# FNet mixer with a gated channel MLP: two rows of statistics written by element-wise DMAs, and four transposes placed elsewhere

## Chip, cores and metric

The kernel runs on one core of a Trainium2 chip. Its metric is the device time in microseconds; the kernel before takes 668.16 us, the median of 3 runs (668.14 to 668.18). Engines: TensorE (matmuls, with its weight loads shown on a line of their own), VectorE, ScalarE, GpSimd, and SyncE (SP), which here does nothing but issue DMAs.

## What is computed

The input x has 2048 tokens of 512 channels. It is normalized over the channels (xn); s is the real part of a two-dimensional DFT of xn (channels, then sequence); g is the SiLU of an MLP of the normalized xn; the output is x + s * g.

```python
def _A_ref(x, dft_seq_re, dft_seq_im, dft_hid_re, dft_hid_im):
    a = jnp.einsum("bsd,ed->bse", x, dft_hid_re)
    b = jnp.einsum("bsd,ed->bse", x, dft_hid_im)
    return jnp.einsum("ts,bse->bte", dft_seq_re, a) - jnp.einsum("ts,bse->bte", dft_seq_im, b)

def _B_ref(x, w1, b1, w2, b2):
    y = _layernorm(x, axis=-1)
    h = _gelu(jnp.einsum("bsd,df->bsf", y, w1) + b1)
    return jnp.einsum("bsf,fd->bsd", h, w2) + b2

xn = _layernorm(x, axis=-1)
s = _A_ref(xn, A_dft_seq_re, A_dft_seq_im, A_dft_hid_re, A_dft_hid_im)
g = _silu(_B_ref(xn, B_w1, B_b1, B_w2, B_b2))
return x + s * g
```

All is float32; D = 512 channels, S = 2048 tokens, F = 1792 hidden units.

## The kernel before

**Numbers as two parts.** Every float32 operand of a matmul is split into a high part, rounded by ScalarE (hi), and a remainder, subtracted by VectorE (lo). A product is three matmuls: hi hi, hi lo, lo hi. Names ending in h and l in the profile are these parts.

**Stages.** First the DFT over the channels for 16 tiles of 128 tokens (accumulators pd, later q with seven products in place of eight for the second half of the tokens), then the MLP (h, then m), then the DFT over the sequence (p), which ends with the gate and the output. The change lies in the first stage, in the first 50 us; matmuls of that stage are recorded at L364 and L349 (pd) and L556 (q).

**The first stage.** Tokens are taken as four blocks of 512, in the order of `TB`. In a block of four tiles (i = 0 to 15) the channels have to lie along the partitions. Tiles 0 to 3 are loaded with their tokens along the partitions, centred there (`first_centre`) and turned by TensorE, four transposes a tile into one bank pt (`first_transpose`, L272), which ScalarE rounds (L64) and VectorE subtracts from (L65). The other blocks are loaded already transposed (xT). What has to be subtracted or multiplied there differs along the free axis, so a row of 512 values, the same on all 128 partitions, is wanted: the means of block 1 (row m1), the negated means of blocks 2, 3 and 0 (row n), and the inverse deviations, called factors (row R).

**How a row is made.** The statistics come out as columns, one value per token with the tokens along the partitions: `nm` holds 12 such columns, `rr` 32, of which R takes 16. `rows_turn` (L170) lets TensorE transpose the columns (L174, 128 x n into n x 128 in a bank rp), ScalarE copy the bank (L176, into the one buffer rt) and issue a DMA to DRAM (L178), n rows of 512 bytes. `row_load` (L180) has SP load 512, 1024 or more values of that DRAM row to all partitions (L182). The second kind of user is `centred_load` (L333): SP loads row n twice a tile (L338) and GpSimd adds the transposed input to it by an accumulating DMA (L339); this is for block 0, which the MLP uses again.

**Order.** The program's order is the order of each engine. `dft_mm(i, m)` issues 12 matmuls of tile i with the real (m = 0) or the imaginary (m = 1) matrix; its argument `mid` is called after `at` of them. Before the change the turn of R is called after two matmuls of `dft_mm(5, 0)`, that of n between `dft_mm(4, 0)` and `dft_mm(4, 1)`, and the transposes of tile 3 (the fourth) after eight matmuls of `dft_mm(2, 0)`. The turn of m1 stands ahead of `dft_mm(2, 0)`. `dft_out` has ScalarE scale an accumulator into a buffer e (L375) and puts its store on a list; SP stores (L386) lag four entries behind.

**Users of the rows.** In the loop over the tiles i = 3 to 7, `second_factors` computes `rr` at i = 4 (L132 last); `a_sums` (L501 to L504) and `last_factors` run on VectorE at i = 5; at i = 6 `y_centre` (L477) adds row n to four tiles xT, and at i = 7 `y_scale` (L480) multiplies two of these by row R; ScalarE rounds them to y_1h (L79) and VectorE makes y_1l (L83). The first of the q products (`q_product(1)`, L556) reads the first y as its weights.

**Buffers.** 39 of 4 KB a partition are shared by most of this (`operand`, `guest`), and eight banks of PSUM hold accumulators, transposes and turns.

Of the kernel before, what the change touches and what calls it, by code (L numbers as in the profile page):

```python
# [8 lines left out]
F32 = mybir.dt.float32  # L9
# [3 lines left out]
AF = mybir.ActivationFunctionType  # L13
ALU = mybir.AluOpType

P = 128
# [6 lines left out]
def fnet_mixer_kernel(ctx: ExitStack, tc: tile.TileContext, x, xT, ct, wt, w1, w2, b1, b2, out):  # L23
    nc = tc.nc
# [3 lines left out]
    NK = D // P  # L28
# [9 lines left out]
    dram = ctx.enter_context(tc.tile_pool(name="dram", bufs=1, space=bass.MemoryType.DRAM))  # L38
# [7 lines left out]
    def operand(name):  # L46
        return op.tile([P, 2, W], F32R, tag="op", name=name)
# [5 lines left out]
    def guest(name):  # L53
        return op.tile([P, 2, W], F32, tag="op", name=name)

    def bank(name):
        return psum.tile([P, W], F32, tag="ps", name=name)
# [5 lines left out]
    def split_into(hi, lo, src):  # L63
        nc.scalar.activation(hi, src, AF.Copy)  # L64
        nc.vector.tensor_sub(lo, src, hi.bitcast(F32))  # L65
# [37 lines left out]
    HB = NS // 2  # L103
    rr = consts.tile([P, 4 * HB], F32, name="rr")
# [4 lines left out]
    nm = consts.tile([P, 3 * NC], F32, name="nm")  # L109
# [6 lines left out]
    def stats(mv, t, i):  # L116
        st = small.tile([P, 6], F32, tag="st", name="st")
        nc.vector.bn_stats(st, t)
        nc.vector.bn_aggr(mv[:, i, :], st)
# [28 lines left out]
    def second_factors():  # L148
        for make, at in ((outer, 0), (inner, HB)):
            make(vv[:, at:at + NC], mv1[:, HB:HB + NC, 1], 1.0)  # L150
            make(vv[:, at + NC:at + HB], sq, 1.0 / D)
        rsqrt(rr[:, 2 * HB:], vv, 2 * HB)

    def last_factors():
        nc.vector.tensor_mul(qq, vv[:, :HB], rr[:, 2 * HB:3 * HB])
        nc.vector.tensor_mul(qq, qq, rr[:, 3 * HB:])
        nc.vector.tensor_scalar(nq, qq, -1.0, None, op0=ALU.mult)


    row_st, row_d = {}, {}  # L160
# [9 lines left out]
    def rows_turn(key):  # L170
        st = row_st[key]
        n = st.shape[1]
        ps = bank("rp" + key)
        nc.tensor.transpose(ps[:n, :P], st, ident)  # L174
        sb = small.tile([n, P], F32, tag="rt", bufs=1, name="rt" + key)
        nc.scalar.activation(sb, ps[:n, :P], AF.Copy)  # L176
        row_d[key] = dram.tile([1, n * P], F32, name="rd" + key)
        nc.scalar.dma_start(out=row_d[key].rearrange("a (b p) -> (a b) p", p=P), in_=sb)  # L178

    def row_load(key, n, at=0):  # L180
        t = guest(f"row{key}_{at}")
        nc.sync.dma_start(out=t.rearrange("p a w -> p (a w)")[:, :n * W],  # L182
                          in_=row_d[key][0, at * W:(at + n) * W].partition_broadcast(P))
        return [t[:, q, :] for q in range(n)]
# [23 lines left out]
    def parts(i):  # L208
        return 1 if i else 2

    def x_load(i):
        if i % 2 == 0:
            x_two[i // 2] = guest(f"x{i}")
        xs[i] = x_two[i // 2][:, i % 2, :]
        nc.sync.dma_start(out=xs[i], in_=x[tok(i) * P:(tok(i) + 1) * P, :])
# [5 lines left out]
    def load_w(m, k2):  # L221
        t = room(f"rw{m}{k2}")
        for k in (2 * k2, 2 * k2 + 1):
# [8 lines left out]
                        in_=wt[:, :, 0:P:8, 0:4].rearrange("m k p w -> p (m k) w"))  # L232
# [13 lines left out]
    xt = {}  # L246
# [18 lines left out]
    def first_transpose(i):  # L265
        t = operand(f"xt{i}")
        hi, lo = t[:, 0, :], t[:, 1, :]
        n = D // parts(i)
        for q in range(parts(i)):
            pt = bank(f"pt{i}{q}")  # L270
            for k in range(NK // parts(i)):
                nc.tensor.transpose(pt[:, k * P:(k + 1) * P], xc[i][:, q * n + k * P:q * n + (k + 1) * P], ident)  # L272
            split_into(hi[:, q * n:(q + 1) * n], lo[:, q * n:(q + 1) * n], pt[:, :n])
        for k in range(NK):
            xt[i, k] = (hi[:, k * P:(k + 1) * P], lo[:, k * P:(k + 1) * P])

    xtr = {}

# [33 lines left out]
    def m_turn():  # L312
        rows_turn("m1")
        mrow[1], = row_load("m1", 1)
# [4 lines left out]
    def neg_means(b):  # L319
        nc.vector.tensor_scalar(nm[:, block(NEG[b])], mv1[:, block(b), 0], -1.0, None, op0=ALU.mult)  # L320
# [3 lines left out]
    def act_stats(i):  # L324
        if not squares:
            squares.append(guest("squares"))
        t, = squares
        c = i % NC
        nc.scalar.activation(t[:, 0, :], xs[i], AF.Copy, scale=-1.0 / D, accum_out=nm[:, NC + c:NC + c + 1])
        nc.scalar.activation(t[:, 1, :], xs[i], AF.Square, bias=nm[:, NC + c:NC + c + 1], accum_out=sq[:, c:c + 1])  # L330
# [12 lines left out]
    def dft_mm(i, m, mid=None, at=2 * NK):  # L343
        acc = bank(f"pd{i}_{m}")
        terms = [(0, 0, k) for k in range(NK)] + [(1, 0, k) for k in range(NK)] + [(0, 1, k) for k in range(NK)]
        for n, (px, pw, k) in enumerate(terms):
            if mid and n == at:
                mid()
            nc.tensor.matmul(acc, xt[i, k][px], weights[m * NK + k][pw], start=n == 0, stop=n == len(terms) - 1)  # L349
        dacc[i, m] = acc  # L350
# [20 lines left out]
    def dft_out(i, m):  # L371
        if m == 0:
            e_two[i] = guest(f"e{i}")
        e = e_two[i][:, m, :]
        nc.scalar.activation(e, dacc.pop((i, m)), AF.Copy, scale=(nr1 if m else rr)[:, i:i + 1])  # L375
        stores.append((dft_at(i, m), e))
        while len(stores) > LAG:
            store()
# [11 lines left out]
    round_w(0)  # L390
    rest_w(0)
    first_transpose(0)
    for n in (1, 2, 3, 4, 5):
        round_w(n)
# [11 lines left out]

    idle_mm(1)
    first_mm(lambda: first_transpose(1))
    first_mean(2)
    first_var(1)  # L410
    first_centre(2)
    stats(mv1, xs[NC], NC)
    stats(mv1, xs[NC + 1], NC + 1)
    dft_mm(1, 0, mid=lambda: first_transpose(2))
    first_mean(3)
    first_var(2)
# [4 lines left out]
    m_pack()  # L421
    dft_mm(1, 1)
    m_turn()
    for q in (14, 15, 10, 11):
        x_load(q)
    for q in (12, 13):
# [1 line left out]
    first_factors()  # L428
    for q in (8, 9):
        stats(mv1, xs[q], q)  # L430
    dft_mm(2, 0, mid=lambda: first_transpose(3))
    dft_out(0, 0)
    dft_out(0, 1)
    dft_out(1, 0)
# [6 lines left out]
    def xt_prepare(b):  # L441
        for k in range(NK // 2):
            xt_centre(b, k)
        for k in range(NK // 2):
            xt_make(b, k)
# [30 lines left out]
    def y_centre(b, k2):  # L476
        nc.vector.tensor_add(xtr[b, k2], xtr[b, k2], both(mrow[b]))  # L477

    def y_scale(k2, b):
        nc.vector.tensor_mul(xtr[b, k2], xtr[b, k2], both(rrow[b]))  # L480
        y_raw[f"{k2 + 1}{b % 2 + 1}", b // 2] = xtr[b, k2]

    def y_round(name, tau):
        y_op[name, tau] = rounded(y_raw[name, tau], f"y{name}_{tau}")

    def y_rest(name, tau):
        rest(y_op[name, tau], y_raw[name, tau])
# [11 lines left out]
    def a_sums():  # L499
        a11, a12, a21, a22 = (room_w[m, k2] for m in range(2) for k2 in range(2))  # L500
        nc.vector.tensor_add(a22, a21, a22)  # L501
        nc.vector.tensor_sub(a21, a11, a21)
        nc.vector.tensor_sub(a11, a22, a11)
        nc.vector.tensor_sub(a12, a12, a11)  # L504
# [60 lines left out]
                for o in do:  # L565
                    o()

    def turn_r():
        row_st["R"] = rr[:, HB:3 * HB]
        rows_turn("R")  # L570

    for i in range(3, HB):
        if i == 3:
            xt_prepare(1)
            for q in (14, 15):
                act_stats(q)
            for q in (10, 11):
                stats(mv1, xs[q], q)
            neg_means(2)
            neg_means(0)  # L580
        if i == 4:
            second_factors()
        if i == 5:
            a_sums()
            last_factors()
        if i == 6:
            for b in (2, 3):
                for k2 in range(2):
                    y_centre(b, k2)
        if i == 7:  # L590
            y_scale(0, 2)
            y_round("11", 1)
            y_scale(1, 2)
            y_round("21", 1)
            y_rest("11", 1)
            y_rest("21", 1)
        dft_mm(i, 0, mid=turn_r if i == 5 else None, at=2)
        if i == 5:
            rrow = [None] * 2 + row_load("R", 2, 2)
        dft_out(i - 1, 1)  # L600
        if i == 4:
            row_st["n"] = nm
            rows_turn("n")
            mrow[2], mrow[3] = row_load("n", 2)
        dft_mm(i, 1)
        dft_out(i, 0)
    dft_out(HB - 1, 1)
# [330 lines left out]
    at = {"load": 0, "sum": 0, "split": 0}  # L938
# [104 lines left out]
    for u, (p, j) in enumerate(m_units):  # L1043
# [3 lines left out]
        if u == 1:  # L1047

            n = NJ - 1
# [5 lines left out]
        n = NJ - 1  # L1055
# [9 lines left out]
        q = m_order.index(p)  # L1065
# [181 lines left out]
```

## Time and profile before

| what | value |
|---|---|
| median of 3 runs | 668.16 us |
| the profiled execution, its time | 668.18 us |
| its span on the core | 666.4 us |
| TensorE busy | 660.5 us, 99% |
| VectorE busy | 541.8 us, 81% |
| ScalarE busy | 357.5 us, 54% |
| GpSimd busy | 50.8 us, 8% |
| DMA | 172.28 MB, mean 259 GB/s |

The span goes from the first to the last instruction; the 1.8 us between it and the time lie around it. Busy time is a sum over the whole span. PE is TensorE's matmuls, PEld its weight loads, which overlap them; DVE is VectorE, ACT ScalarE, POOL GpSimd; a q behind an engine's name is its queue, which waits and issues DMAs. The chain of waits lists work in order, each piece ending where the next begins; the order of time lists instructions by start and duration, like ones merged with their count. In a window's row the engines' busy times are followed by TensorE's granted clock, the mean busy share of the 16 DMA engines and GB/s. In a DMA queue's row stand packets, MB and the time that the packets took, as a share of 16 engines over the window.

### The profile page before, as it was taken

Reading aid. Unit: us, or ns where it says so; the run is one execution under the profiler, and the core shown is the slowest. Engines: PE = TensorE matmul, PEld = TensorE weight load, DVE = VectorE, ACT = ScalarE, POOL = GpSimd, SP = SyncE. Lnnn points to the kernel's source line nnn. Section 1 sums busy time; section 2 is a strip of 40 time slices with the busy share of each in tenths; the row PEclk is TensorE's granted clock in tenths of the full one; section 3 lists DMA queues with packets and bytes.
Section 4 is the critical chain, followed back from the end, with each engine's and each line's share of the span. In section 5 each row is a group of like instructions: output and inputs, shape, how many; then the busy total and the mean of one; then the engine's idle time right before and its main releaser. Section 6 shows DMA issues by size and latency. Waiting matters only on the chain.

```text
span 666.4 us, 8214 instructions
## 1 busy us (share of the span) xinstructions
PE 660.5 (99%) x2926; PEld 544.3 (82%) x2926; DVE 541.8 (81%) x590; ACT 357.5 (54%) x407; POOL 50.8 (8%) x84
## 2 busy tenths in 40 slices
PE   9999999999999999999999999999999999999997
PEld 5788888888888888888888888888888888888886
DVE  6899878867777866888979998739877299898996
ACT  6745657544456655555455544456544455646540
POOL 0002000321222100000000000000000001210100
PEclk9999999999999999999999999999999999999999
DMA  9778260887989999798799996416544558996983
GB/s 329 263 267 224 88 235 1 316 312 284 333 302 352 417 413 360 268 391 282 279 397 409 360 340 221 152 52 203 187 154 128 127 139 253 301 248 236 336 253 129
DMA packets 70761, 172.28 MB, mean 259 GB/s; under 512 B 6816, under 2 KB 21696, under 8 KB 70720
## 3 DMA queue, kind: packets, MB, share of 16 engines
q1 hardware_dynamic: 58480, 131.88, 56.1%
q0 software_dynamic: 12032, 39.86, 19.2%
q8 instruction: 23, 0.38, 0.2%
q14 instruction: 18, 0.15, 0.1%
q10 hardware_dynamic: 208, 0.02, 0.0%
HBM read 121.38 MB, written 50.35 MB: 258 GB/s over the span
## 4 chain that ended last, share of the span: by engine, by line
PE 99%; DMA 0%; DVE 0%; issue 0%
PE pz L861 20%; PE px L861 18%; PE ma L861 11%; PE hy L676 11%; PE mb L861 9%; PE pd L349 6%; PE hz L676 6%; PE pw L861 5%; PE qy L556 3%; PE hx L676 3%; PE px L1182 2%; PE pw L1182 2%; PE qz L556 2%; PE pd L364 1%; PE qx L556 1%; DMA x<-x 0%
## 5 line engine op out<-in xcount | busy, mean ns | idle before, releaser
L967 DVE TENSOR_TENSOR c<-c,c 128x1024 f32<-128x1024 f32 x32 | 39.0, 1219 | 4.1 <-DMA c<-ct 4.1
L83 DVE TENSOR_TENSOR w1l<-w1r,w1h 128x1792 fp32r<-128x1792 f32 x7 | 14.2, 2025 | 21.6 <-ACT w1h L463 21.6
L65 DVE TENSOR_TENSOR R_b1l<-c,R_b1h 128x1024 fp32r<-128x1024 f32 x16 | 19.4, 1221 | 14.9 <-ACT R_b1h L64 11.6
L681 ACT ACTIVATE hc<-hc,b_t 128x1024 f32<-128x1024 f32 (+1 forms) x18 | 17.3, 960 | 25.2 <-DVE hc L721 22.6
L861 PE MATMUL pw<-R_s1h,L 128*128 128x512 f32 x96 | 29.7, 389 | 0.0
L64 ACT ACTIVATE R_s3h<-c 128x1024 fp32r<-128x1024 f32 x16 | 17.0, 1061 | 23.6 <-DVE c L967 8.0
L64 ACT ACTIVATE R_b2h<-c 128x1024 fp32r<-128x1024 f32 x16 | 16.9, 1056 | 18.5 <-DVE c L972 14.1
L65 DVE TENSOR_TENSOR R_s2l<-c,R_s2h 128x1024 fp32r<-128x1024 f32 x16 | 19.6, 1222 | 8.6 <-PE pz L861 8.6
L64 ACT ACTIVATE R_s2h<-c 128x1024 fp32r<-128x1024 f32 x16 | 17.0, 1061 | 16.8 <-PE px L861 9.3
L64 ACT ACTIVATE R_b1h<-c 128x1024 fp32r<-128x1024 f32 x16 | 16.7, 1052 | 15.1 <-DMA c<-ct 9.1
L65 DVE TENSOR_TENSOR R_s3l<-c,R_s3h 128x1024 fp32r<-128x1024 f32 x16 | 19.5, 1220 | 4.0 <-PE pz L861 4.0
L64 ACT ACTIVATE R_s1h<-c 128x1024 fp32r<-128x1024 f32 x16 | 16.4, 1051 | 11.7 <-DVE c L978 9.7
L975 POOL DMA_DIRECT2D c<-ct x8 | 7.0, 873 | 202.4 <-DVE c L972 161.8
L64 ACT ACTIVATE R_a1h<-c 128x1024 fp32r<-128x1024 f32 x16 | 16.9, 1054 | 8.9 <-PE pz L861 7.2
L861 PEld LDWEIGHTS pw<-R_s1h,L 128*128 128x128 f32 x96 | 18.0, 188 | 3.7
L65 DVE TENSOR_TENSOR R_b2l<-c,R_b2h 128x1024 fp32r<-128x1024 f32 x16 | 19.4, 1219 | 1.5 <-PE px L861 1.5
L65 DVE TENSOR_TENSOR R_a1l<-c,R_a1h 128x1024 fp32r<-128x1024 f32 x16 | 19.5, 1220 | 1.3 <-PE px L861 1.1
L64 ACT ACTIVATE R_s4h<-c 128x1024 fp32r<-128x1024 f32 x16 | 16.8, 1049 | 6.4 <-PE pz L861 5.0
L65 DVE TENSOR_TENSOR R_s4l<-c,R_s4h 128x1024 fp32r<-128x1024 f32 x16 | 19.5, 1219 | 0.7 <-PE px L861 0.7
L972 DVE TENSOR_TENSOR c<-c,c 128x1024 f32<-128x1024 f32 x16 | 19.6, 1223 | 0.4
L64 ACT ACTIVATE w2h<-w 128x1024 fp32r<-128x1024 f32 (+1 forms) x14 | 13.2, 945 | 11.5 <-DVE w L789 3.9
L65 DVE TENSOR_TENSOR R_s1l<-c,R_s1h 128x1024 fp32r<-128x1024 f32 x16 | 18.8, 1218 | 0.1
(954 smaller groups left out, 2224.2 us busy)
## 6 DMA issues: line engine op xcount, KB each, us to landing
c<-ct SPq DMA_DIRECT2D x68, 512.0 KB, 5.6
m<-h_d SPq DMA_DIRECT2D x48, 512.0 KB, 6.9
h_d<-ht POOLq DMA_DIRECT2D x21, 512.0 KB, 5.9
s_d<-sa SPq DMA_DIRECT2D x32, 256.0 KB, 4.1
la<-s_d SPq DMA_DIRECT2D x32, 256.0 KB, 5.5
h_d<-hc POOLq DMA_DIRECT2D x13, 512.0 KB, 3.7
x<-x SPq DMA_DIRECT2D x16, 256.0 KB, 5.5
sa<-a_d SPq DMA_DIRECT2D x8, 512.0 KB, 5.7
```

The costliest lines, as they stand in the source:

```text
L64: nc.scalar.activation(hi, src, AF.Copy)
L65: nc.vector.tensor_sub(lo, src, hi.bitcast(F32))
L83: nc.vector.tensor_sub(hi_lo[1], src, hi_lo[0].bitcast(F32))
L349: nc.tensor.matmul(acc, xt[i, k][px], weights[m * NK + k][pw], start=n == 0, stop=n == len(terms) - 1)
L556: nc.tensor.matmul(qx[key, c], a, w, start=p in (1, 5, 2) and n == 0, stop=p in (2, 3, 4) and n == len(terms) - 1, skip_group_check=True)
L676: nc.tensor.matmul(acc[:, tau, :], w[:, W1_AT[p], k * P:(k + 1) * P], r[:, k, :], start=p in (1, 5, 2) and i == 0, stop=p in (2, 3, 4) and ...
L681: nc.scalar.activation(dst, src, AF.Gelu_apprx_tanh, bias=b1_t[:, row:row + 1])
L861: nc.tensor.matmul(acc[k][:, tau, :], a, c[:, tau, :], start=first and i == 0, stop=last and i == len(terms) - 1, skip_group_check=True)
L967: nc.vector.tensor_sub(t, t, raw)
L972: nc.vector.tensor_add(raw, raw, t)
L975: nc.gpsimd.dma_start(out=t, in_=ct[1, 1, n], accum_op=ALU.add)
L1182: nc.tensor.matmul(acc[KEY[name]][k][:, tau, cols], a[k], c[:, tau, cols], start=False, stop=last and u == us[-1] and i == 2, skip_group_c ...
```

## The change

A new function `rows_send` writes columns to the row in DRAM directly: one DMA, issued by SP, whose source is the columns in SBUF (128 partitions x n values) and whose target is the DRAM row seen with a step of 128 values, so that each 4-byte value goes to a place of its own. Rows n and R are written so; their turns, `turn_r` and the two calls of `rows_turn`, go. R is sent directly behind the load of row n, in the loop at i = 4; its 16 columns come from instructions that stand ahead of it in VectorE's order; its loads stay where they were. `rows_turn` stays for m1.

`first_transpose(3)` is called behind `m_turn()`, ahead of `dft_mm(2, 0)`, instead of inside it. It issues the transposes and ScalarE's rounding there; for this tile it returns the subtraction on VectorE, which is issued behind `dft_mm(2, 0)`, where it was in VectorE's order.

```diff
+    def rows_send(key, cols):
+        n = cols.shape[1]
+        row_d[key] = dram.tile([1, n * P], F32, name="rd" + key)
+        nc.sync.dma_start(out=row_d[key].rearrange("a (b p) -> p (a b)", p=P), in_=cols)
...
     def first_transpose(i):
         t = operand(f"xt{i}")
         hi, lo = t[:, 0, :], t[:, 1, :]
+        for k in range(NK):
+            xt[i, k] = (hi[:, k * P:(k + 1) * P], lo[:, k * P:(k + 1) * P])
         n = D // parts(i)
         for q in range(parts(i)):
             pt = bank(f"pt{i}{q}")
             for k in range(NK // parts(i)):
                 nc.tensor.transpose(pt[:, k * P:(k + 1) * P], xc[i][:, q * n + k * P:q * n + (k + 1) * P], ident)
-            split_into(hi[:, q * n:(q + 1) * n], lo[:, q * n:(q + 1) * n], pt[:, :n])
-        for k in range(NK):
-            xt[i, k] = (hi[:, k * P:(k + 1) * P], lo[:, k * P:(k + 1) * P])
+            nc.scalar.activation(hi[:, q * n:(q + 1) * n], pt[:, :n], AF.Copy)
+            if i == 3:
+                return lambda: nc.vector.tensor_sub(lo, pt, hi.bitcast(F32))
+            nc.vector.tensor_sub(lo[:, q * n:(q + 1) * n], pt[:, :n], hi[:, q * n:(q + 1) * n].bitcast(F32))
...
     m_turn()
+    rest_3 = first_transpose(3)
     for q in (14, 15, 10, 11):
         x_load(q)
...
-    dft_mm(2, 0, mid=lambda: first_transpose(3))
+    dft_mm(2, 0)
+    rest_3()
     dft_out(0, 0)
...
-    def turn_r():
-        row_st["R"] = rr[:, HB:3 * HB]
-        rows_turn("R")
...
-        dft_mm(i, 0, mid=turn_r if i == 5 else None, at=2)
+        dft_mm(i, 0)
         if i == 5:
             rrow = [None] * 2 + row_load("R", 2, 2)
         dft_out(i - 1, 1)
         if i == 4:
-            row_st["n"] = nm
-            rows_turn("n")
+            rows_send("n", nm)
             mrow[2], mrow[3] = row_load("n", 2)
+            rows_send("R", rr[:, HB:3 * HB])
         dft_mm(i, 1)
         dft_out(i, 0)
```

## The prediction

> **What bounds the kernel now.** I read first the page's head, then the chain of waits between 4 and 60 us, then the waits of the weight loads, then the order of time of each engine from 32 to 53 us, and last the DMA windows. The page says that TensorE is the bound everywhere:
>
> ```profile
> span 666.4 us, 8214 instructions
> ...
> PE 660.5 (99%) x2926; PEld 544.3 (82%) x2926; DVE 541.8 (81%) x590; ACT 357.5 (54%) x407; POOL 50.8 (8%) x84
> ```
>
> So only what the change takes off TensorE, or makes TensorE wait for, can move the end. The chain (start us, us, what) shows where the pieces concerned stand; all of its rows here are TensorE's, one directly behind the other:
>
> ```profile
> 18.68 0.23 PE rpm L174
> 18.92 1.83 PE pd L349 x8
> 20.75 0.44 PE pt L272 x4
> 21.18 11.81 PE pd L349 x52
> 33.00 0.24 PE rpn L174
> 33.24 3.20 PE pd L349 x14
> 36.44 0.11 PE rpR L174
> 36.55 15.91 PE pd L349 x70
> 52.46 5.44 PE qy L556 x24
> ```
>
> The reader is to see three things. A matmul at full pace costs 5.44 / 24 = 0.2267 us. The four transposes of a tile cost 0.44, 0.11 each. A turn costs 0.11 (rpR), 0.23 or 0.24; the dearer two waited for what they turn, of which the waits of the weight loads show
>
> ```profile
> PEld rpm L174 <- DVE rsm L166: 0.4, 1, 0.4
> ```
>
> And behind each interruption the matmuls run a little long: 1.83 - 8 x 0.2267 = 0.02, 11.81 - 52 x 0.2267 = 0.02, 3.20 - 14 x 0.2267 = 0.03, 15.91 - 70 x 0.2267 = 0.04 us.
>
> **Taken off TensorE.** The turn of the negated means (rpn) goes with its wait and its slow tail: 0.24 + 0.03 = 0.27 us. The turn of the factors (rpR): 0.11 + 0.04 = 0.15 us. Nothing behind them in the chain waits for anything but TensorE, so both come off the end: 0.42 us.
>
> A chain row is not an instruction's duration:
>
> ```profile
> L174 PE MATMUL rpn<-ident,nm x1: 269/269/269, 33.0 to 33.0; 128*12 128x128 f32 x1
> ```
>
> The turn lasts 0.269 us and overlaps its neighbours. The Trainium skill, page "TensorE: Matmul & The Clock Gate", Part 4, states about 275 ns for a transpose in a kernel's context; the trace agrees as to the duration. Put into the sum in place of the chain's 0.24 and 0.11, two such durations would make the gain 0.64 us, an estimate from that page; I stay with the chain.
>
> **Moved on TensorE.** The four transposes of tile 3 stand 8 matmuls earlier, directly behind the turn rpm. They cost their 0.44 as before; one interruption in place of two saves one tail, 0.02 us. Before, the first accumulator of block row 2 (pd) was allotted at this very place and began without a wait, so I take no wait for the transposes' bank either. If they were given the bank of rpm itself, they would wait for ScalarE's copy of it:
>
> ```profile
> 18.95 0.27 ACT L176 ACTIVATE rtm<-rpm 4x128 f32<-4x128 f32 x1 [1.43 <-PE rpm L174]
> ...
> 22.73 0.58 ACT L64 ACTIVATE xt<-pt 128x512 fp32r<-128x512 f32 x1
> ...
> 34.49 0.30 ACTq L178 DMA_DIRECT2D rdn<-rtn  x1
> ...
> 37.09 0.36 ACTq L178 DMA_DIRECT2D rdR<-rtR  x1
> ...
> 47.23 2.20 ACT L79 ACTIVATE y_1h<-xT 128x1024 fp32r<-128x1024 f32 x2 [2.21 <-DVE xT L480]
> ```
>
> That is until 19.22 instead of 18.92, so the ends of this edit are -0.05 and +0.3 us. The rounding of tile 3 (22.73 above) moves on ScalarE ahead of the squares of tiles 12 and 13, which come 0.6 us later and end together about when the rounding ended; their sums are first used behind the row nm of 32.58 below. The remainder on VectorE stays in place. Tile 3 is first multiplied 16 matmuls behind its old place (21.18 + 16 x 0.2267 = 24.8), so an earlier rounding gains nothing.
>
> **Taken off ScalarE.** Two copies and two DMA issues go. ScalarE is 54% busy and off the path, so I count nothing.
>
> **Added: two element-wise DMAs on SP.** The negated means are 128 partitions x 12 values, 1536 pieces of 4 bytes; the factors 128 x 16, 2048 pieces. Over 16 DMA engines that is 96 and 128 pieces each. Before, they were 12 and 16 pieces of 512 bytes. What a piece costs is the unknown of this case. The nearest rows are those of ScalarE's queue in two windows, from 2.6 to 4.2 us (128 loads of 16 bytes and 16 semaphore words) and from 39.0 to 40.6 us (16 rows of 512 bytes and 16 words):
>
> ```profile
> q10 hardware_dynamic: 144, 0.00, 5.0%
> ...
> q10 hardware_dynamic: 32, 0.01, 2.2%
> ```
>
> 5.0% of 16 x 1.6 us over 144 is 8.9 ns for a tiny piece; 2.2% over 32 is 17.6 ns in the mean, so a 512-byte row takes about 26. I take 8.9, the row whose size is nearest (none writes 4 bytes to DRAM), with 26 as the upper end. A wave of n then takes 0.85 us, one of R 1.14 us.
>
> SP is in order, and the chain through it is what can hurt. SP's rows, then VectorE's:
>
> ```profile
> 28.91 0.32 SPq L386 DMA_DIRECT2D b_d<-e  x1
> 36.73 0.32 SPq L182 DMA_DIRECT2D rown<-rdn  x1
> ...
> 40.83 0.32 SPq L182 DMA_DIRECT2D rowR<-rdR  x1
> ```
>
> ```profile
> 32.58 0.24 DVE L320 TENSOR_SCALAR nm<-mv 128x4 f32<-128x4 f32 x2
> ...
> 35.95 0.17 DVE L132 SCALAR_TENSOR_TENSOR rr<-tv,y 128x16 f32<-128x16 f32 x1
> ...
> 41.43 4.63 DVE L477 TENSOR_TENSOR xT<-xT,rown 128x1024 f32<-128x1024 f32 x4
> 45.98 2.35 DVE L480 TENSOR_TENSOR xT<-xT,rowR 128x1024 f32<-128x1024 f32 x2
> 48.33 2.36 DVE L83 TENSOR_TENSOR y_1l<-xT,y_1h 128x1024 fp32r<-128x1024 f32 x2
> ```
>
> After its store at 28.91 SP stands idle until the row n has landed. With the change it issues n as soon as nm is there, 32.87, two DMAs and 1.6 us sooner than ScalarE did (34.49). But now n is behind SP's own stores and loads, which fill the engines (the share of DMA stands ahead of the GB/s at the end):
>
> ```profile
> 34.50:35.00 0.50, 0.50 (x4) 0.42 (x3) 0.43 (x3) 0.00 (x0) 0.00 (x0) 1.00 1.05 402
> ...
> 35.50:36.00 0.50, 0.50 (x4) 0.42 (x3) 0.40 (x3) 0.34 (x1) 0.00 (x0) 1.00 0.48 174
> 36.00:36.50 0.50, 0.50 (x4) 0.32 (x4) 0.50 (x2) 0.00 (x0) 0.00 (x0) 1.00 0.07 26
> ```
>
> So its pieces run from about 35.5 to 36.4 and, with the 0.6 us that lie between the last pieces of the old transfer (about 36.1, the 0.07 above) and SP's next issue (36.73), n lands at 37.0, 0.3 later than before. The broadcast load of n is issued at 37.0, R (ready at 36.12) right behind it at 37.4. The loads landed
>
> ```profile
> DMA to landing us min/median/max: 3.9/3.9/3.9
> ...
> DMA to landing us min/median/max: 4.4/5.1/5.8
> ```
>
> after their issue (n's; R's first was the 4.4). So n's load is there at 40.9, when VectorE is still busy (it adds n from 41.43, without idling), and costs nothing. R's pieces stand behind that load's data, from about 40.3 to 41.4, and land at 42.0; SP then issues the load of R at 42.05 instead of 40.83, and it lands at 46.45. The multiplication by R begins at 46.5 instead of 45.98.
>
> What covers this: TensorE's first products with the results,
>
> ```profile
> 52.07 0.41 PEld L556 LDWEIGHTS qy<-W,y_1h 128*128 128x128 f32 x2
> 52.53 0.19 PEld L556 LDWEIGHTS qy<-W,y_1l 128*128 128x128 f32 x1
> ```
>
> come 0.44 us earlier than here, at 51.63 and 52.09. The high parts are ready at 48.3 (half of the 2.20 above), the first low part at 49.5. The low part is the tighter: 2.55 us. The multiplication may slip to 48.5, so R may land at 44.05; I expect 42.0. The margin is 2.05 us, and each further nanosecond a piece costs 96 + 128 = 224 of them: TensorE waits once a piece takes over 8.9 + 9.2 = 18 ns.
>
> **Issue time, and what queues behind it on SP.** A DMA of 128 pieces takes SP 0.32 us, one of 256 pieces 0.51:
>
> ```profile
> L182 SPq DMA_DIRECT2D rowR<-rdR x2: 319/450/580, 40.8 to 46.1; - x2
> ...
> L763 SPq DMA_DIRECT2D s_d<-sa x32: 512/519/1169, 160.8 to 329.8; - x32
> ```
>
> That is 1.5 ns a piece, an estimate of 2.4 us for n (32.9 to 35.3, behind the backlog) and 3.2 us for R (37.4 to 40.6, behind n's load). The stores of block rows 2 to 4, until now from 37.14 on, come up to 4 us later; only their buffers wait for them. Cost nothing, unless the pool runs dry.
>
> **Sum.** 668.18 (the profiled execution) - 0.27 - 0.15 - 0.02 = 667.74 us; the median 668.16 is 0.02 lower, so 667.7 us, 0.07% less. 0.2%, 1.34 us, is about what a measurement of this kernel tells from no change.
>
> **Rivals.** (1) Slow pieces: R is late and TensorE stands before its first product with y. It decides from 18 ns a piece. At 26 ns: 224 x 17.1 ns = 3.8, less 2.05, is 1.8 us, so 669.5, the first to be slower by 0.2%; at 50 ns 7.2 us, so 674.9. For it: pieces of neighbouring partitions fall into the same few bytes of DRAM, which no row shows. Against it: packets of 4 and 16 bytes alike took 8.9 ns. The Trainium skill, page "DMA: Bandwidth & Descriptors", speaks against the change: a strided last dimension "lowers to one descriptor per element" (Rules for kernel authors), and below 512 bytes the engine reads, modifies and writes (Specifications). What that would do here can be priced by the accumulating DMAs, which read their target too, from 56 to 62 us, against plain ones from 28 to 33 us:
>
> ```profile
> q0 software_dynamic: 447, 0.88, 84.0%
> ...
> q1 hardware_dynamic: 1028, 1.98, 105.2%
> ```
>
> 180 against 82 ns a packet, 2.2 times: a piece of 20 ns, 0.4 us over the margin, 668.1 us.
> (2) No gain: the transposes wait for rpm's bank (+0.3), or a piece near 20 ns eats it: 668.0 to 668.2. The chain, unbroken, speaks against it.
> (3) A larger gain: more than the two turns, their tails and 0.05 is not on TensorE to be had; 667.6, and anything beyond needs what the profile doesn't show.
>
> **Chances.** Forecast 0.70 (its own range 667.55 to 668.1), rival 1 0.17 (0.15 of it slower by over 0.2%), rival 2 0.10, rival 3 0.03, which I count as faster though only half believed. So faster 0.03, same 0.82, slower 0.15. The range goes from 667.4 to 669.6, with the 26 ns case in it and the dearer ones left out.
>
> **What would show it.** Right: no rpn and rpR rows, one unbroken piece of pd matmuls from the first row's turn to the first qy, four transposes directly behind rpm, qy beginning 0.44 us earlier, the load of R issued between 41 and 44, no TensorE wait at qy. Wrong: a wait of qy for y_1h or y_1l, R landing after 44, or a wait of the transposes for ScalarE.

## The result, and the profile after

The changed kernel takes 683.37 us, the median of 5 runs (682.83 to 683.47), against 668.16 for the kernel before (5 runs, 668.14 to 668.90). The ratio is 1.0225, with a 95% interval of 1.0214 to 1.0236: it is slower by 15 us. The prediction was 667.7, and its range ended at 669.6. The profiled execution took 682.83 us, 14.65 more than that of before.

The head of the page after, with the rows of TensorE's work and of its granted clock in 40 slices of 17 us. The fourth slice, from 51 to 68 us, is new: in it TensorE stands, and its clock is down.

```profile
span 681.1 us, 8203 instructions
...
PE 663.2 (97%) x2924; PEld 545.8 (80%) x2924; DVE 542.1 (80%) x590; ACT 357.6 (53%) x405; POOL 50.8 (7%) x84
...
PE   9993999999999999999999999999999999999997
...
PEclk9996999999999999999999999999999999999999
```

The chain of waits after (start us, us, what). qy, qx and qz are the accumulators of the q products, hy, hz and hx those of the MLP's first products. Before, all rows of the chain from 18 to 60 us were TensorE's. Now it leaves TensorE behind the turn rpm, at 18.90, and comes back only at 63.78; from 32.65 on its way leads through the two new DMAs:

```profile
18.63 0.27 PE rpm L174
...
32.65 10.48 DMA rdn<-nm
...
43.15 0.32 SPq L187
...
43.56 13.02 DMA rdR<-rr
...
56.64 4.67 DMA rowR<-rdR
...
61.41 1.24 DVE xT L490
...
62.67 1.07 ACT y_1h L79
...
63.78 1.22 PE qy L566 x2
...
65.03 6.75 PE qy L566 x22
71.79 5.44 PE qx L566 x24
...
104.47 0.70 ACT q L549
...
105.21 1.67 PE hy L682 x6
106.88 1.38 PE hz L682 x6
```

The write of n lasts 10.48 us from issue to landing, that of R 13.02, and the second is issued only when the first has landed, because SP waits with the load of n, which stands between them. The waits of TensorE after (us in total, times, longest) name what this costs, and a second place:

```profile
PE qy L566 <- ACT y_1h L79: 11.8, 1, 11.8
...
PE hy L682 <- ACT q L549: 0.8, 1, 0.8
```

From these rows the 15 us can be put together:

- The wait of qy for its first y: 11.8 us.
- The first 24 products with y end at 71.79, 8.01 us after they began, where the kernel before took 5.44: 2.6 us.
- At hy, the wait and the slow first matmuls: 105.21 is 0.77 behind the end of q (104.44), and six matmuls take 1.67 instead of 6 x 0.2267 = 1.36: 1.1 us.
- The gain: qy could have begun at 63.78 - 11.8 = 52.0 instead of 52.46: 0.5 us.

Together 15.0, which is also how much later TensorE's last matmul stands; what lies behind that matmul was 0.35 us shorter in this execution.

Why the first products are slow is told by the windows of the profile after (in a row: PE, PEld, DVE, ACT, POOL, granted clock, DMA share, GB/s):

```profile
54.00:56.00 2.00, 0.00 (x0) 0.00 (x0) 0.00 (x0) 0.00 (x0) 0.00 (x0) 0.63 0.26 14
56.00:58.00 2.00, 0.00 (x0) 0.00 (x0) 0.00 (x0) 0.00 (x0) 0.00 (x0) 0.50 0.01 2
...
66.00:68.00 2.00, 2.00 (x6) 1.56 (x5) 1.97 (x3) 1.54 (x3) 0.00 (x0) 0.50 1.00 304
68.00:70.00 2.00, 2.00 (x9) 1.60 (x9) 2.00 (x3) 1.45 (x2) 0.00 (x0) 0.95 0.82 164
```

TensorE stands from 52.0; its clock falls to 0.50 between 54 and 56 (in half-microsecond windows it is still 1.00 until 54.5, so after 2.5 us of standing) and is back shortly after 68, some 4.4 us after the work began again. By the Trainium skill, page "TensorE: Matmul & The Clock Gate", Part 1, the clock is halved after an idle window of about 3.4 us and returns after about as much work. This trace agrees that it is halved and returns; its two times are 2.5 and 4.4 us.

Then the place of the delay within the DMAs. The order of time of SP after:

```profile
32.65 0.37 SPq L183 DMA_DIRECT2D rdn<-nm  x1
43.15 0.32 SPq L187 DMA_DIRECT2D rown<-rdn  x1
43.56 0.39 SPq L183 DMA_DIRECT2D rdR<-rr  x1
44.00 2.91 SPq L394 DMA_DIRECT2D a_d<-e  x1
56.64 0.32 SPq L187 DMA_DIRECT2D rowR<-rdR  x1
```

The DMA window from 32.6 to 43.2 us, first the busy tenths of the 16 engines in 40 slices of 0.27 us, then the issue with its size and time to landing:

```profile
DMA  9999999999996320500000000000000000000000
...
rdn<-nm SPq DMA_DIRECT2D x1, 6.0 KB, 10.5
```

By 36.9 the engines had gone through everything given to them, the 1536 pieces among it. Then for 6 us no engine shows any work, and the transfer had still not landed. The window from 43.5 to 56.7 us, with R and the store behind it:

```profile
DMA  0097499999949996983998049876936242421100
...
a_d<-e SPq DMA_DIRECT2D x1, 256.0 KB, 13.8
```

Here the engines are not quiet. R's pieces pass between 46 and 48 us, 8.6 us before R has landed; what fills the row from 48 to 56 is the store behind it, 88 packets in all, which take 64.7% of the 16 engines, some 0.95 us each, where the prediction has 82 ns for a plain packet. The store took 13.8 us; in the kernel before, such stores (a_d) between 28 and 50 us took 6.1 in the median. It is off the path, but it shows that what stands behind such a write is held up too.

The other half of the change did as forecast. TensorE's order of time after:

```profile
18.61 0.27 PE L174 MATMUL rpm<-ident,rsm 128*4 128x128 f32 x1
18.72 0.60 PE L279 MATMUL pt<-ident,xc 128*128 128x128 f32 x4
19.08 11.15 PE L357 MATMUL pd<-W,xt 128*128 128x512 f32 x48
```

The transposes follow the turn of the first row by 0.11 us, without a wait, and rpn and rpR are gone.

### The profile page after: what moved, and what is told of

Its sections match the earlier page's. It is cut to its first block, busy times and chain, and to the rows that moved or that the text cites. A ratio compares the mean times of both kernels' runs of the same rounds, so it can differ in the third digit from the quotient of the medians.

```text
span 681.1 us, 8203 instructions
## 1 busy us (share of the span) xinstructions
PE 663.2 (97%) x2924; PEld 545.8 (80%) x2924; DVE 542.1 (80%) x590; ACT 357.6 (53%) x405; POOL 50.8 (7%) x84
## 4 chain that ended last, share of the span: by engine, by line
PE 93%; DMA 5%; ACT 1%; DVE 1%; issue 0%; SPq 0%; DVEq 0%
PE pz L867 19%; PE px L867 18%; PE hy L682 11%; PE ma L867 11%; PE mb L867 8%; PE hz L682 6%; PE pw L867 5%; PE qy L566 4%; PE hx L682 3%; DMA rdR<-rr 2%; PE px L1188 2%; PE pw L1188 2%; PE qz L566 2%; DMA rdn<-nm 2%; PE pd L372 1%; PE pd L357 1%
## 5 line engine op out<-in xcount | busy, mean ns | idle before, releaser
L64 ACT ACTIVATE R_s1h<-c 128x1024 fp32r<-128x1024 f32 x16 | 16.4, 1051 | 11.3 <-DVE c L984 11.3
L64 ACT ACTIVATE R_b1h<-c 128x1024 fp32r<-128x1024 f32 x16 | 16.7, 1053 | 10.5 <-DMA c<-ct 4.5
```

## The experiments

The theory after the result: it is not the DMA engines that need long for a piece; 16 neighbouring partitions write into the same 64 bytes of DRAM, and such writes wait for one another behind the engines. The rival: a cost per piece, whatever its place. A second question is the wait at hy, which stands 40 us behind the change.

**Either half alone.** The changed kernel with the transposes at their old place (rows_only):

```diff
-    rest_3 = first_transpose(3)
...
-    dft_mm(2, 0)
-    rest_3()
+    dft_mm(2, 0, mid=lambda: first_transpose(3)())
```

> The changed kernel with the fourth tile's transposes put back inside the first product of tile 2; both rows still sent as 4-byte pieces. Theory 'the rows carry the loss': about 683.4 us like the changed kernel (it loses at most the 0.02 us of a merged interruption). Rival 'the moved transposes share in it' (a wait for a bank, another order on ScalarE): 1 us or more under the changed kernel.

Measured: 684.18 us, ratio 1.0238 (1.0223 to 1.0254). n landed 11.0 us after its issue, R 14.0, and qy waited 13.1 us for y_1h.

The kernel before with the transposes moved and the turns kept (transposes_only):

```diff
-            rows_send("n", nm)
+            row_st["n"] = nm
+            rows_turn("n")
             mrow[2], mrow[3] = row_load("n", 2)
-            rows_send("R", rr[:, HB:3 * HB])
```

> The kernel before with only the fourth tile's transposes moved behind the first row's turn; both other turns stay. Theory 'the rows carry the loss': 668.1 us, 0.02 to 0.1 under the kernel before, no wait of TensorE. Rival 'the moved transposes share in the loss': over 668.5 us.

Measured: 668.22 us, ratio 1.0000 (0.9991 to 1.0009), and no new wait of TensorE. The whole loss is in the rows; the 0.02 us that the forecast gave to the transposes are below what these runs can tell.

**The pieces by themselves.** Behind the outputs of the kernel before, eleven DMAs of one kind after the other, with nothing else on the chip (pieces). The times of this kernel and of the next such one hold these additions; only the landings count.

```diff
+    send(spread(12, 1), pb[:, 0, :12, None])                # 4 bytes, side by side
+    send(spread(12, 16)[:, :, 0:1], pb[:, 0, :12, None])    # 4 bytes, 64 apart
+    send(spread(12, 16), pb[:, 0, :192].rearrange("p (b w) -> p b w", w=16))   # 64 bytes
```

> The kernel before with eleven small DMAs behind its end, each waiting until the one before it has landed, from SP, nothing else moving; its time is longer by their sum. All but two write zeros from SBUF to a scratch place in DRAM. In order: (1) 128 pieces of 48 bytes; (2) 1536 pieces of 4 bytes laid as row n is, so that 16 neighbouring partitions share 64 bytes; (3) 768 such pieces; (4) 1536 of 4 bytes, each 64 bytes apart; (5) 512 bytes apart; (6) 1536 of 4 bytes, 8 bytes apart, the 12 of a partition side by side; (7) 1536 of 4 bytes from 8 partitions, 192 each; (8) 1536 of 16 bytes; (9) 1536 of 64 bytes; (10) a load of 1536 pieces of 4 bytes; (11) 1536 pieces of 4 bytes from SBUF to SBUF. In the changed kernel row n landed some 7.3 us and row R 9.9 us after their first pieces began, 4.8 ns for each piece of all engines together, though the engines were done with the pieces after 1.5 us. Theory 'shared places': the memory takes writes into the same 64 bytes one after the other; then (2) 9 us, (3) 5.5, (4) and (5) about 3, (6) between. Theory 'every small write': any 4-byte write to DRAM costs the memory 4.8 ns wherever it goes; then (2), (4), (5), (6) and (7) all 9 us, (3) 5.5, (11) about 3. Theory 'engine': each engine waits 76 ns for the answer to each write; then (7), on 8 engines, about 16 us, and (8) and (9) as slow as (2). For all of them (1) 2 to 2.5 us, and (10) about 3.

The DMA window of the write that is like row n (1536 pieces of 4 bytes, side by side), 11.2 us in slices of 0.28 us; the last row is its time from issue to landing:

```profile
DMA  0001777010000000000000000000000000000000
...
q1 hardware_dynamic: 1552, 0.01, 6.2%
...
pr<-pb SPq DMA_DIRECT2D x1, 6.0 KB, 11.0
```

The engines are busy for 1.1 us and idle for 9: 6.2% of 16 x 11.2 us over 1552 packets is 7.2 ns a piece. With as many pieces of 64 bytes each (2.4 us from 717 on, slices of 0.06 us):

```profile
DMA  0000000000018999888888888983000000000000
...
pr<-pb SPq DMA_DIRECT2D x1, 96.0 KB, 2.5
```

Sixteen times the bytes and not a quarter of the time. And the 4-byte pieces again, 64 bytes apart:

```profile
pr<-pb SPq DMA_DIRECT2D x1, 6.0 KB, 3.5
```

The others, each 1536 pieces from partitions to DRAM unless said otherwise, us from issue to landing:

| pieces | us |
|---|---|
| 128 of 48 bytes | 1.4 |
| 4 bytes, side by side (as row n) | 11.0 |
| 768 of the same | 10.4 |
| 4 bytes, 64 apart | 3.5 |
| 4 bytes, 512 apart | 3.2 |
| 4 bytes, 8 apart, each partition's 12 next to one another | 9.2 |
| 4 bytes, side by side, from 8 partitions of 192 | 9.6 |
| 16 bytes, side by side | 4.5 |
| 4-byte reads into SBUF | 2.4 |
| 4-byte writes from SBUF to SBUF, 8 apart within each partition | 2.6 |

Half the pieces take 95% of the time, and a step of 64 bytes takes away two thirds of it. So it is the place that counts most: against 'every small write' stand the 3.5 and 3.2 us of pieces set apart, against 'engine' the 9.6 us of 8 partitions, for which it had some 16. But 'shared places' had 5.5 us for 768 pieces, not 10.4.

**How many share a place.** A second such kernel with eight other DMAs (sharing):

```diff
+    send(spread(1, 1), pb[:, 0, :1, None])                  # 128 pieces
+    send(spread(12, 2)[:, :, 0:1], pb[:, 0, :12, None])     # 4 bytes, 8 apart
+    send(spread(12, 4)[:, :, 0:1], pb[:, 0, :12, None])     # 16 apart
```

> The kernel before with eight small DMAs behind its end, each waiting for the one before, zeros from SBUF to a scratch place in DRAM, as in the run of the eleven. (1) 128 pieces of 4 bytes side by side, one a partition: 16 pieces in each 64 bytes, 8 such places. (2) 24 columns laid as row n, 3072 pieces; (3) 16 columns, 2048 pieces as row R; both 16 in each 64 bytes. (4) 1536 pieces 8 bytes apart, 8 in each 64 bytes; (5) 16 bytes apart, 4; (6) 32 bytes apart, 2; neighbours always from neighbouring partitions. (7) 1536 pieces of 32 bytes side by side. (8) 12 pieces a partition, 8 bytes apart within 128 bytes of its own, so that one engine alone writes each place. Theory 'one place after another', 0.56 us for each piece that shares a place beyond the first: (1), (2), (3) all 10 to 11 us, (4) 6.5, (5) 4.3, (6) and (7) 3.2, (8) 6 to 9. Theory 'one queue', 4.8 to 7 ns for each sharing piece: (1) 3 us, (2) 17 to 23, (3) 12 to 16, (4), (5), (6) and (8) 9 to 11.

The DMA window around its first two, 128 pieces in one column and 3072 in 24:

```profile
pr<-pb SPq DMA_DIRECT2D x1, 0.5 KB, 7.1
pr<-pb SPq DMA_DIRECT2D x1, 12.0 KB, 17.2
```

For 1536 pieces by how many fall into the same 64 bytes: 1, 3.5 us; 2, 4.2; 4, 4.6; 8, 6.6; 16, 11.0. With 16 sharing, by number: 128, 7.1 us; 768, 10.4; 1536, 11.0; 2048, 12.4; 3072, 17.2. Of these 1536 and 2048 are the rows n and R; in the changed kernel they took 10.5 and 13.0, so it is not in the main the traffic around them that makes them late. With 8 sharing, it made no difference whether a place's pieces come from neighbouring partitions or from one (6.9); the 9.2 in the table above, where each partition's 12 take 96 bytes, stays unexplained. So most is there with 128 pieces already, and some comes with the number: neither "one place after another" nor "so much a piece" alone, though the first is far the nearer. 1536 pieces of 32 bytes side by side, two in each 64, took 2.55 us, no longer than pieces of 64; so whether a place is 64 bytes or 32 isn't settled, and the counts above are counts by 64. Which part of the chip holds the writes apart isn't seen either.

**Changing the order.** R sent before the load of n instead of behind it (both_first):

```diff
             rows_send("n", nm)
-            mrow[2], mrow[3] = row_load("n", 2)
             rows_send("R", rr[:, HB:3 * HB])
+            mrow[2], mrow[3] = row_load("n", 2)
```

> The changed kernel with row R sent directly behind row n, ahead of the load of n, so at about 36.2 us instead of 43.6. Row n still lands at about 43.1. Theory 'one place after another' (a place of 64 bytes takes its writes one by one, some 0.6 us each, all places at once; the time hangs on how many pieces share a place, not on how many pieces there are): R lands some 10 us after its issue, about 47, its load at 51.5, y_scale then waits for y_centre; TensorE waits about 3 us, 671 to 674 us. Theory 'one queue' (the memory or the engines work off all these pieces in one line, 4.8 ns each): R lands after n and 10 us more, 53 to 54, TensorE waits 8 to 9 us, 678 to 680 us.

Measured: 682.21 us, ratio 1.0210 (1.0192 to 1.0229); qy waited 10.8 us. SP's order of time:

```profile
32.86 0.37 SPq L183 DMA_DIRECT2D rdn<-nm  x1
36.12 0.37 SPq L183 DMA_DIRECT2D rdR<-rr  x1
47.40 0.33 SPq L187 DMA_DIRECT2D rown<-rdn  x1
...
51.36 0.32 SPq L187 DMA_DIRECT2D rowR<-rdR  x1
```

The two writes overlap, so R lands 5.2 us earlier. But n lands 4.2 us later, and its load, issued at 47.40 while R is under way, is used only from 56.03, after 8.6 us instead of 3.9: what R gains is lost again on n, which VectorE needs first. Neither theory had this time (671 to 674, 678 to 680).

Eight columns of each row sent first, and the rest later (half):

```diff
+            rows_send("n", nm, 0, 8)
             mrow[2], mrow[3] = row_load("n", 2)
+            rows_send("R", rr[:, HB:3 * HB], 8, 16)
```

> The changed kernel with only the first needed columns sent in the old places: 8 of n (1024 pieces) and 8 of R (1024 pieces); the other 4 and 8 follow behind the first load of R. Theory 'one place after another': landings as in the changed kernel, R at 55 to 57, 682 to 684 us. Theory 'one queue': n lands at about 40.5 and R at about 48, TensorE waits 3 to 4 us, 672 to 675 us.

Measured: 682.88 us, ratio 1.0220 (1.0201 to 1.0239); 1024 pieces of n took 11.1 us, 1024 of R 12.7, and qy waited 11.9. Fewer pieces help nothing, as in the probes and as 'one place after another' had it (682 to 684).

**The clock.** The changed kernel with 54 idle matmuls ahead of its first product with y, so that TensorE does not stand (fill). The expectation names the kernel before, but it is the changed kernel that got the idle matmuls, so its 679.8 to 680.4 says nothing here.

```diff
+    idle_mm(54)
```

> The changed kernel's stall is left as it is... in this run the kernel before gets 54 idle matmuls (bf16, 128x512) ahead of its first product with y, work that is not in the reference's sum. It shows what such a filling costs by itself where TensorE does not wait: 54 x 0.216 = 11.7 us by the pace of 0.2267 us at most 12.2 us, so 679.8 to 680.4 us; rival: they are partly absorbed later, under 679.

Measured: 682.65 us, ratio 1.0215 (1.0201 to 1.0229), beside 684.18 for rows_only and 683.37 for the change. The clock stays at 1.00 between 50 and 80 us, and TensorE's waits are now:

```profile
PE qy L566 <- ACT y_1h L79: 0.9, 1, 0.9
PE qy L566 <- DVE y_1l L83: 0.5, 1, 0.5
```

The first 24 products take 6.6 us instead of 8.0, yet the median is only 0.7 us lower, which the two intervals don't tell from nothing. qy begins 1.0 us later (R landed later in this execution), and 1.2 us are lost anew between 78 and 82 us, where the chain runs through VectorE, which stood for R too and is behind with its work; at hy TensorE doesn't wait in this version, 1.1 us. -1.4 + 1.0 + 1.2 - 1.1 is -0.3, the distance of the two profiled executions (682.49 and 682.83). So the halved clock is real, 1.4 of the 2.6 us, but without it most of this price goes to VectorE.

**The wait at hy.** The rows turned by VectorE in blocks of 32 x 32, and written by four DMAs a row in pieces of 128 bytes (dve_turn): the change's purpose without its small pieces.

```diff
+    def rows_block(key, wide):
+        turned[key] = consts.tile([P, 32], F32, name="tb" + key)
+        nc.vector.transpose(turned[key], wide)
...
+        to = row_d[key].rearrange("a (c b r) -> b (a c) r", b=4, r=32)
+        for b in range(4):
+            nc.sync.dma_start(out=to[b], in_=turned[key][32 * b + at:32 * b + at + n, :])
```

> The kernel before with the turns of n and R taken off TensorE in another way: VectorE transposes the columns in blocks of 32 x 32 (one instruction a row of statistics), and SP writes the blocks, four DMAs of 12 or 16 pieces of 128 bytes each. No two pieces share 64 bytes. The fourth tile's transposes stay where they were. Theory 'the small shared pieces are the loss': rows land at about 36.7 (n) and 40.5 (R) as in the kernel before, TensorE never waits, and the two turns come off: 0.42 us under the kernel before. Rival 'any write of less than 512 bytes is slow': R lands after 44 and TensorE waits, over 669 us.

Measured: 672.71 us, ratio 1.0068 (1.0054 to 1.0082). There is no wait left in the first stage, and the loads of n and R are issued at 36.85 and 41.48, close to where they were (36.73 and 40.83). But hy waits, as in the changed kernel:

```profile
PE hy L688 <- ACT q L553: 0.8, 1, 0.8
```

and between 91 and 233 us the matmuls come every 233 ns instead of 226.7, 3.9 us in all. So there are two more losses that need no slow row.

The first: rpn and rpR each took a bank of PSUM out of a rotation of eight. In the kernel before the last accumulator of q lies in bank 3; with two fewer it lies in bank 0, where the MLP's first accumulator, hy, always goes, and hy waits until ScalarE has read it. (The banks are those of the built programs; the profile doesn't show them. With the idle matmuls of the version above it is bank 6, and hy didn't wait there.) Two banks held by a one-element memset put it back into bank 3. In the changed kernel (after_banks):

```diff
+    def hold(name):
+        nc.vector.memset(bank(name)[:1, :1], 0.0)
...
-        dft_mm(i, 0)
+        dft_mm(i, 0, mid=(lambda: hold("rpR")) if i == 5 else None, at=2)
...
         if i == 4:
+            hold("rpn")
             rows_send("n", nm)
```

> The changed kernel, with two PSUM banks taken by a one-element memset of VectorE where rpn and rpR took theirs, so that the last q accumulator no longer lies in the bank that the MLP's first accumulator uses (bank 3 as in the kernel before, not bank 0). Bank theory: the wait of hy for ScalarE's q (0.8 us, with its tail some 1.1 us together) is gone and nothing else changes: about 682.3 us, still 14 us above the kernel before. Rival, that the wait at hy is a late consequence of the stall at qy (the order of evacuations pushed back by it): the wait stays, 683.4 us.

Measured: 683.10 us, ratio 1.0222 (1.0208 to 1.0236). The wait of hy is gone. The time can't tell it: in this execution qy waited 12.7 us instead of 11.8. The same two memsets in dve_turn (dve_turn_banks):

> The rows turned by VectorE in 32x32 blocks and written in pieces of 128 bytes, and two PSUM banks taken by one-element memsets where rpn and rpR took theirs. Bank theory: no wait at hy, the pace of the products behind it 226.7 ns instead of 233 from 91 to 233 us, and what is left is the gain of the removed turns, 0.4 us: 667.7 to 667.8 us, ratio 0.9993 to 0.9994. If the slow pace has nothing to do with the wait: 667.8 + 3.8 = 671.6 us. If the wait isn't from the bank: 672.7 us as without the memsets.

Measured: 671.64 us, ratio 1.0051 (1.0038 to 1.0063), 1.1 us less than without them, and no wait of hy; the slow pace stays. Then the kernel before with six memsets, placed so that q ends in bank 0 (before_shift), and six placed so that it ends in bank 7 (before_shift_else):

```diff
     for i in range(3, HB):
+        for q in range({4: 1, 5: 1, 6: 2, 7: 2}.get(i, 0)):
+            hold(f"d{i}{q}")
```

> The kernel before with its turns, and six PSUM banks taken for a moment by one-element memsets of VectorE (one each at the start of tiles 4 and 5, two each at 6 and 7), which moves the last q accumulator into bank 0, where the MLP's first accumulator goes. Bank theory: hy waits for ScalarE's q, 0.8 to 0.9 us, so 669.2 to 669.4 us without the slow pace, about 673 us with it. Rival, that the wait comes from the rows being sent in another way: no wait, 668.2 us.

> The control of the one before: six memsets too, but two at tile 5 and one at tile 6, which puts the last q accumulator into bank 7. Bank theory: no wait at hy, 668.2 us. If the memsets themselves cost something, both controls are dearer alike.

Measured: 669.16 us, ratio 1.0015 (1.0006 to 1.0023) with bank 0, and 668.23, ratio 1.0001 (0.9992 to 1.0010) with bank 7. Bank 0 brings the wait of the changed kernel into the kernel before:

```profile
PE hy L681 <- ACT q L539: 0.8, 1, 0.8
```

and the control has none. That settles the wait at hy. The Trainium skill, page "Perfetto Trace Analysis", section "Matmuls", asks that independent groups of matmuls rotate through different banks; this is what it costs here where two of them meet, 1.0 us.

**The slow pace.** dve_turn has 320 bytes more of constants on each partition, so the split weights w1h begin at 188864, 64 bytes past a multiple of 128, instead of 188544. (These places, too, are those of the built programs; the profile doesn't show them.) The kernel before with 64 bytes of constants more (before_odd), and dve_turn_banks with 64 bytes more, w1h at 188928 (dve_turn_even):

```diff
+    pad = consts.tile([P, 16], F32, name="pad")
+    nc.gpsimd.memset(pad, 0.0)
```

> The kernel before with 64 bytes of constants more and nothing else, so that the split weights lie 64 bytes past a multiple of 128 (188608 instead of 188544). Place theory: 233 ns a matmul in the MLP's first products, 3.8 us more: 672.0 us, ratio 1.0057. Rival: 668.2 us.

> The rows turned by VectorE, the banks set right, and 64 bytes of constants more in each partition, so that the split weights of the MLP lie on multiples of 128 bytes again (188928 instead of 188864). Place theory: the pace of the MLP's first products is 226.7 ns and what is left is the gain of the removed turns, 0.4 us: 667.7 to 667.8 us, ratio 0.9993 to 0.9994. Rival, that the slow pace comes from the transposes of VectorE or the eight small transfers: 671.6 us as without the 64 bytes.

Measured: before_odd 671.95 us, ratio 1.0057 (1.0045 to 1.0070); dve_turn_even 670.93, ratio 1.0042 (1.0029 to 1.0056). The chain of before, and then that of before_odd, at the same work:

```profile
199.34 5.44 PE hy L676 x24
```

```profile
202.47 5.60 PE hy L678 x24
```

64 unused bytes make the products with these weights 2.9% slower; those of q, m and p keep their pace in all these versions. A multiple of 128 was not the whole rule, as dve_turn_even shows with 232 ns a matmul: 188544 lies 128 past a multiple of 256, 188928 on one. With 192 bytes more w1h begins at 189056, again 128 past a multiple of 256 (dve_turn_place):

```diff
-    pad = consts.tile([P, 16], F32, name="pad")
+    pad = consts.tile([P, 48], F32, name="pad")
```

> The rows turned by VectorE, the banks set right, and 192 bytes of constants more, so that the split weights begin 128 bytes past a multiple of 256, as in the kernel before (189056 and 188544). Place theory: 226.7 ns a matmul throughout, no wait, and the gain of the removed turns is left by itself: 667.7 to 667.8 us, ratio 0.9993 to 0.9994. Rival, that the transposes of VectorE or the small transfers slow these products too: 670.9 us or more, as with 64 bytes.

Measured: 667.54 us, the median of 11 runs, against 668.21 of 15; ratio 0.9989 (0.9980 to 0.9998). It is faster than the kernel before, if only by a tenth of a per cent. Its chain:

```profile
18.68 0.23 PE rpm L178
...
21.20 30.85 PE pd L365 x136
52.05 5.44 PE qy L572 x24
```

One unbroken piece of pd where the kernel before had three and two turns between, and qy at 52.05 instead of 52.46; the rest of the 0.7 us lies within the interval. SP sends the same values, in pieces of 128 bytes:

```profile
33.34 1.68 SPq L194 DMA_DIRECT2D rdn<-tbn  x4
37.41 0.35 SPq L198 DMA_DIRECT2D rown<-rdn  x1
37.85 1.76 SPq L194 DMA_DIRECT2D rdR<-tbR  x4
...
41.87 0.34 SPq L198 DMA_DIRECT2D rowR<-rdR  x1
```

Four issues cost SP 1.7 us where one cost 0.37, and both rows are there in time.

## Why the prediction was wrong, point by point

- **Turns taken off TensorE** (0.42 us): right in size. dve_turn_place has qy 0.41 us earlier. "Nothing behind them in the chain waits for anything but TensorE" was wrong: the two turns held two places in the rotation of banks, and hy waited once they were gone, 1.1 us, more than their gain. The forecast looked at banks only for the moved transposes.
- **Transposes moved** (0.02, ends -0.05 and +0.3): right. Directly behind rpm, no wait; alone 1.0000.
- **The step that failed** is the landing of the two writes: "its pieces run from about 35.5 to 36.4 and, with the 0.6 us that lie between the last pieces of the old transfer [...] and SP's next issue [...], n lands at 37.0". The first half held: 7.2 ns a piece in the probe beside 8.9 forecast, and the engines were through by 36.9. The 0.6 us did not carry over. They were taken from rows of 512 bytes, each with places of its own; for 4-byte writes that share 64 bytes it was 6.2 us for n and 8.6 for R (from 48 to 56.6). n landed at 43.13; SP, in order, issued R 6.1 us later than forecast (43.56 instead of 37.4), and R landed 13.0 us after its issue instead of 4.6: at 56.58 instead of 42.0, 14.6 us late. Less the forecast's margins that is 12.5 us of wait for the low part (2.05) and 11.3 for the high part (51.63 - 48.3 = 3.3); 11.8 were measured, and it was the high part that ended the wait, not the low part that the forecast took for the tighter. So the path through SP, VectorE and ScalarE to qy was right, and one term on it, used twice, was off by a factor of ten and more.
- **Rival 1** named the ground, "pieces of neighbouring partitions fall into the same few bytes of DRAM", and set it aside with the engines' time on tiny packets. That row could not speak to it: it gives one mean for 16-byte loads and 4-byte words, not 8.9 ns for each, and an engine's time is not the landing: behind n's last piece the engines showed nothing for 6 us. Its prices (669.5 at 26 ns, 674.9 at 50) were in the wrong unit, nanoseconds a piece.
- **The page weighed in rival 1**, "DMA: Bandwidth & Descriptors" of the Trainium skill, was right that each element becomes a descriptor ("Rules for kernel authors"; 1552 packets are 1536 pieces and 16 words). Its limit of 512 bytes ("Specifications") doesn't tell these cases apart: 64-byte pieces landed in 2.5 us, 4-byte pieces 512 apart in 3.2, side by side in 11.0. The 668.1 made from it was too low by 15.
- **Issue time on SP** (2.4 and 3.2 us): wrong, 0.37 and 0.39 measured. It did not grow with the pieces of these writes, and it cost nothing either way.
- **Stores queued behind SP** (nothing): right; TensorE waits for no buffer.
- **Not in the forecast:** half the clock after a long wait (1.4 of the 2.6 us on the first 24 products). It belongs to the price of a wait this long.
- **What would show it wrong** was named: a wait of qy for y_1h, and R landing after 44. Both came.

## What to carry to other kernels

A DMA's time is from issue to landing, and its engines' busy time is only a part of it: 4-byte writes that lie side by side in DRAM landed 7 to 17 us after issue, though the engines were through with 1536 of them in about one. Turn such columns first, on TensorE as before or on VectorE as in dve_turn_place, so that a piece is 64 bytes or more. And before work is taken out, look at what it holds by being there: a place in a rotation of banks, an address behind it.

## What the runs showed of the hardware that was not expected

- Writes of 4 bytes into shared 64 bytes: from 3.5 us (none shared) to 11.0 (16 shared) for the same 1536 pieces. Reads of the same places took 2.4, and as many 4-byte writes into SBUF 2.6.
- What stands behind them in the DMA queues is held as well: a store of 256 KB took 13.8 us instead of some 6, and a load of a row 8.6 instead of 3.9.
- The place of matmul operands in SBUF can set their pace: 226.7 ns at 128 bytes past a multiple of 256, about 232 on a multiple of 256, 233 at 192 past one. That was seen for the products with w1h and w1l, whose places move together, on five places in all; which of the two matters, and why, stays open.
